# A decode kernel with V as the stationary operand of P times V, and K and V in one pool of 8 KB units

## The chip, the cores and the metric

The kernel runs on one core of one Trainium2 chip. The metric is the device time of one execution in microseconds (us). Before the change the median of three runs was 325.77 us (324.56 to 330.94, the last of them slow); a fourth run makes it 326.71. In what follows PE is the tensor engine (PEld its weight loads), DVE the vector engine, ACT the scalar engine, POOL the GpSimd engine and SP the engine that issues the loads; "SPq" in the profile is SP's own queue of instructions.

Each run is fast or slow; a run over 1.5% above the fastest of the same kernel is slow. The profiled executions of all kernels below had a granted clock of 1.0 for the tensor engine (the share of its full clock that the profile records), with one exception that is named.

## The reference

Two layers, each an attention over a window of the cache and a gated feed-forward block. Both layers use the same weights and the same caches.

```python
def _A_ref(x, k_cache, v_cache, wq, wo):      # x: [4, 1, 448]; 16 query heads, 8 KV heads, Dh = 256
    W = min(4096, max(256, Sk // 4))          # Sk = 8192, so W = 2048
    q = (x @ wq) ...                          # [B, 16, 1, 256]
    k = k_cache[:, :, Sk - W:, :]             # each KV head serves two query heads
    v = v_cache[:, :, Sk - W:, :]
    p = softmax(q k^T * Dh**-0.5)
    return (p v) ... @ wo
def _B_ref(x, w_gate, w_up, w_down):
    return (silu(x @ w_gate) * (x @ w_up)) @ w_down
x = x + _A_ref(layernorm(x)); x = x + _B_ref(layernorm(x))    # and both once more
```

The unit of work is a *pair*: one token and one KV head in one layer, so 4 x 8 x 2 = 64 pairs. A pair needs 1 MB of K and 1 MB of V. For each token five K and five V are kept in SBUF, the on-chip memory, from the first layer to the second; the rest is loaded again. That makes 88 loads of 512 KB of K halves and 88 of V halves, and 104 MB of loads with the weights.

## The kernel before

A scheduler in Python orders the instructions of each engine once, at build time, from a duration for each operation: the second argument of `g.op` (for example 1.18 us for a transpose). At run time each engine works through its list in that order and waits where it has to.

K arrives with keys on the partitions and has to be transposed, because the kernel's score matmuls take it with Dh there. DVE does it in 32x32 blocks of 4-byte words (two bf16 each), 88 instructions of 1233 ns. The parts that matter, for one pair:

```python
NS = 2; NQ = 3; NY = 3                         # buffers of scores, of q, of outputs
half = [sb(f"half{s}", [128, 8 * DH], BF16) for s in range(15)]    # 15 buffers of 4 KB per partition: raw K, or V
KT = [sb(f"KT{s}", [128, 16 * DH], BF16) for s in range(6)]        # 6 buffers of 8 KB: K transposed
# --- K: load two halves, transpose each; runs of 32 words are written side by side ---
src = half[cell[0]][:, :].bitcast(UINT32).rearrange("p (l k s) -> p l k s", l=2, k=16)
dst = KT[ks][:, :].bitcast(UINT32).rearrange("p (k l r) -> p l k r", k=16, l=4)
g.op(DVE, 1.12 + 0.06, pos, ... e.transpose(dst[:, 2 * hf:2 * hf + 2], src) ...)
# --- scores: 32 weight loads of K, 8 columns of q each ---
last = e.matmul(Sb[s_][:, 8 * gg:8 * gg + 8], lhsT=kt[:, gg, ce // 2, ce % 2, :], rhs=qe[q_][:, ce, :, :], ...)
# --- maximum (DVE, PE, DVE), then exp on ACT, once per query head ---
g.op(SCA, 0.17, pos, ... praw[s_] = exp(Sb[s_] - max) ...)
# --- keys are in the order of the transposes; V's rows are in another. A permutation matmul, and a copy ---
g.op(PE, 0.03, pos, lambda e: e.matmul(Yb[p_][:, 64:96], lhsT=permb[:, :], rhs=praw[s_][:, :], ...))
g.op(PE, 0.03, pos, ... matmul with ones: the sum of the weights ...)
g.op(SCA, 0.13, pos, ... pT[p_] = copy of Yb[p_][:, 64:96], every weight twice ...)
# --- P times V: V moves, 256 columns; 16 matmuls, each in a tile of 32 columns ---
last = e.matmul(Yb[p_][32 * gg:32 * gg + 4, 256:512], lhsT=pT[p_][:, 4 * gg + 2 * hv + a, :, :]...,
                rhs=half[vs[hv][0]][:, 1024 * a + 256 * gg:1024 * a + 256 * gg + 256], ...)
# --- o as a bf16 part and what is left of it; a "flip" matmul turns both round and adds up the tiles ---
g.op(SCA, 0.28, pos, ... oh[p_] = copy of Yb[p_][:, 256:512] ...)
g.op(DVE, 0.4, pos, ... oh[p_] = oh[p_] * lomask - Yb[p_][:, 256:512] ...)
last = e.matmul(Yb[p_][:, 2 * dh:2 * dh + 2], lhsT=oh[p_]..., rhs=osel[:, :], ...)        # twice
g.op(DVE, 0.09, pos, ... oT = Yb[p_][:, 0:4] / sum ...)
```

## Time and profile before

| before | value | where it is read |
|---|---|---|
| span of the profiled run | 322.9 us | head of the page |
| PE / DVE / ACT busy | 72% / 60% / 22% | part 1 |
| K transposes | 88 of 1233 ns, 108.3 us | part 5 |
| P times V | 1024 matmuls, 70.0 us | part 5 |
| GB/s in 0-88, 88-274, 274-303 us | 385, 351, 208 | busy time by windows |

The page of the kernel before. The first line is part 1 (busy time, share of the span, instructions); then the GB/s of 40 equal slices of 8.1 us; then the chain of work that ended last, by engine and by line; then five groups of instructions (output<-input, shape, count, busy us, mean ns of one, idle time of the engine before them, and what ended most of it).

```profile
PE 232.6 (72%) x5728; PEld 169.7 (53%) x5728; DVE 192.6 (60%) x608; ACT 72.4 (22%) x289; POOL 84.9 (26%) x199
...
GB/s 277 399 407 392 393 396 397 391 396 397 391 362 308 338 368 346 400 362 309 301 272 373 375 351 405 355 365 339 277 359 377 357 386 391 277 140 305 5 0 5
...
DMA 38%; PE 34%; DVE 12%; SPq 7%; issue 5%; ACT 2%; POOL 0%; DVEq 0%
DMA half<-in_A_k_cache_dram 20%; DMA half<-in_A_v_cache_dram 12%; PE Y L677 11%; PE S L637 8%; DVE KT L617 6%; DMA wd_sb<-in_B_w_down_dram 5%; PE Z L473 4%; SPq L389 4%; PE A L724 3%; PE Z L514 3%; DVE oh L691 2%; PE Z L542 2%; SPq L609 2%; DVE small L652 2%; SPq L626 1%
...
L617 DVE STREAM_TRANSPOSE KT<-half 128x1024 uint32<-128x1024 uint32 x88 | 108.3, 1233 | 13.3 <-DMA half<-in_A_k_cache_dram 12.9
L637 PE MATMUL S<-qe,KT 128*128 128x8 bf16 x2048 | 64.6, 168 | 22.4 <-DVE KT L617 18.5
L677 PE MATMUL Y<-half,pT 128*4 128x256 bf16 x1024 | 70.0, 403 | 9.6 <-DMA half<-in_A_v_cache_dram 8.7
...
L691 DVE SCALAR_TENSOR_TENSOR oh<-oh,small,Y 128x256 bf16<-128x256 bf16 x64 | 30.1, 472 | 23.9 <-ACT oh L689 23.4
...
L697 PE MATMUL Y<-osel,oh 128*128 128x2 bf16 x128 | 13.3, 173 | 17.4 <-DVE oh L691 17.2
```

How to read this. No engine is full. The chain goes through loads, PE and DVE in turn, and the loads run at about 395 GB/s for the first 88 us and then, up to 274 us, between 272 and 405. The four lower groups are what the change aims at: PE waited 18.5 us for transposes ahead of its score matmuls, and 17.2 us for the subtraction of line 691 ahead of the flip, in which it was busy for another 13.3 us; the subtraction itself took DVE 30.1 us.

The same by stages, from the table of windows (stretch in us, its length, then the busy us of PE, PEld, DVE, ACT and POOL with their counts, the granted clock, the share of DMA, GB/s):

```profile
0.00:88.00 88.00, 44.31 (x1019) 31.70 (x1019) 45.82 (x148) 13.12 (x51) 18.14 (x47) 1.00 1.01 385
88.00:274.00 186.00, 148.95 (x3671) 106.85 (x3672) 124.72 (x369) 48.89 (x197) 54.36 (x122) 1.00 0.97 351
274.00:303.00 29.00, 26.15 (x711) 20.89 (x708) 16.01 (x61) 6.96 (x28) 8.71 (x22) 1.00 0.61 208
```

The first stretch is bound by loads (385 GB/s, DMA share 1.01). In the second there is something to win, since loads run at 351 instead of 395 GB/s; in the third PE is busy for 26 of 29 us.

### The profile page before, as it was taken

The numbers are of one execution on the slowest core, as the hardware profiler recorded it, in microseconds if no ns is written. First come the engines' busy times: TensorE is split into PE (matmuls) and PEld (weight loads), VectorE is DVE, ScalarE is ACT, GpSimd is POOL, SyncE is SP. The second block draws the span as 40 slices with busy tenths as digits, with TensorE's granted clock in tenths as the row PEclk, the third lists the DMA queues.
The fourth block names the chain that finished last, engine by engine and source line by source line (L and its number), as shares of the span: only waits on it lengthen the run. The fifth ranks groups of instructions, "written<-read, shape, count | busy, mean of one in ns | idle before, by whom it ended". The sixth has DMA issues, their size and how long they took to land.

```text
span 322.9 us, 12873 instructions
## 1 busy us (share of the span) xinstructions
PE 232.6 (72%) x5728; PEld 169.7 (53%) x5728; DVE 192.6 (60%) x608; ACT 72.4 (22%) x289; POOL 84.9 (26%) x199
## 2 busy tenths in 40 slices
PE   3654454446588788578796895679787959889875
PEld 2542322234476465366664653567555636686554
DVE  5386555652145778765447787855377874656332
ACT  1112111111022333211231322113223322123310
POOL 3312111112023223240233331313233413134221
DMA  7999999999999999999889999999899999748000
GB/s 277 399 407 392 393 396 397 391 396 397 391 362 308 338 368 346 400 362 309 301 272 373 375 351 405 355 365 339 277 359 377 357 386 391 277 140 305 5 0 5
DMA packets 42327, 105.27 MB, mean 326 GB/s; under 512 B 3096, under 2 KB 7200, under 8 KB 41888
## 3 DMA queue, kind: packets, MB, share of 16 engines
q1 hardware_dynamic: 42272, 104.45, 88.0%
q8 instruction: 45, 0.74, 0.9%
q14 instruction: 10, 0.08, 0.1%
HBM read 104.44 MB, written 0.00 MB: 323 GB/s over the span
## 4 chain that ended last, share of the span: by engine, by line
DMA 38%; PE 34%; DVE 12%; SPq 7%; issue 5%; ACT 2%; POOL 0%; DVEq 0%
DMA half<-in_A_k_cache_dram 20%; DMA half<-in_A_v_cache_dram 12%; PE Y L677 11%; PE S L637 8%; DVE KT L617 6%; DMA wd_sb<-in_B_w_down_dram 5%; PE Z L473 4%; SPq L389 4%; PE A L724 3%; PE Z L514 3%; DVE oh L691 2%; PE Z L542 2%; SPq L609 2%; DVE small L652 2%; SPq L626 1%
## 5 line engine op out<-in xcount | busy, mean ns | idle before, releaser
L617 DVE STREAM_TRANSPOSE KT<-half 128x1024 uint32<-128x1024 uint32 x88 | 108.3, 1233 | 13.3 <-DMA half<-in_A_k_cache_dram 12.9
L637 PE MATMUL S<-qe,KT 128*128 128x8 bf16 x2048 | 64.6, 168 | 22.4 <-DVE KT L617 18.5
L677 PE MATMUL Y<-half,pT 128*4 128x256 bf16 x1024 | 70.0, 403 | 9.6 <-DMA half<-in_A_v_cache_dram 8.7
L637 PEld LDWEIGHTS S<-qe,KT 128*128 128x128 bf16 x2048 | 59.7, 104 | 30.7 <-DVE KT L617 20.8
L687 POOL TENSOR_TENSOR small<-small 128x2 f32<-128x2 f32 x64 | 44.3, 696 | 113.5 <-DVE small L669 103.3
L656 ACT ACTIVATE praw<-S,small 128x16 bf16<-128x16 f32 x128 | 28.7, 279 | 84.6 <-DVE small L652 83.9
L691 DVE SCALAR_TENSOR_TENSOR oh<-oh,small,Y 128x256 bf16<-128x256 bf16 x64 | 30.1, 472 | 23.9 <-ACT oh L689 23.4
L689 ACT ACTIVATE oh<-Y 128x256 bf16<-128x256 f32 x64 | 24.6, 384 | 74.2 <-PE Y L677 74.2
L641 POOL TENSOR_TENSOR qe<-qc,qmask 128x64 bf16<-128x64 bf16 x64 | 18.6, 294 | 71.3 <-PE S L637 52.3
L677 PEld LDWEIGHTS Y<-half,pT 128*4 128x4 bf16 x1024 | 20.0, 94 | 21.8 <-DMA half<-in_A_v_cache_dram 11.5
L646 DVE TRANSPOSE_TENSOR_REDUCE pmax<-S 128x1 bf16<-128x32 f32 x64 | 13.4, 211 | 27.1 <-PE S L637 25.3
L724 PE MATMUL A<-oT,wo_sb 128*128 128x1 bf16 (+1 forms) x688 | 24.8, 166 | 6.4 <-DVE oT L702 6.1
L724 PEld LDWEIGHTS A<-oT,wo_sb 128*128 128x128 bf16 x688 | 22.2, 105 | 10.5 <-DVE oT L702 8.5
L697 PE MATMUL Y<-osel,oh 128*128 128x2 bf16 x128 | 13.3, 173 | 17.4 <-DVE oh L691 17.2
L652 DVE TENSOR_REDUCE small<-S 128x2 f32<-128x128 f32 x64 | 17.4, 282 | 10.4 <-PE S L649 8.3
L666 ACT ACTIVATE pT<-Y 128x64 bf16<-128x64 f32 x64 | 14.1, 222 | 40.7 <-PE Y L663 40.4
L697 PEld LDWEIGHTS Y<-osel,oh 128*128 128x128 bf16 x128 | 8.8, 111 | 27.0 <-DVE oh L691 24.5
L649 PE MATMUL S<-identb,pmax 128*128 128x128 bf16 x64 | 16.6, 284 | 4.5 <-DVE pmax L646 3.6
L473 PE MATMUL Z<-xn,wq_sb 128*128 128x1 bf16 (+1 forms) x480 | 15.6, 165 | 2.6 <-DMA wq_sb<-in_A_wq_dram 1.9
L473 PEld LDWEIGHTS Z<-xn,wq_sb 128*128 128x128 bf16 x480 | 14.3, 104 | 3.4 <-DMA wq_sb<-in_A_wq_dram 2.0
L669 DVE TENSOR_REDUCE small<-Y 128x2 f32<-128x32 f32 x64 | 11.0, 177 | 7.1 <-ACT pT L666 6.8
L440 POOL TENSOR_SCALAR st<-st 128x1 f32<-128x1 f32 x16 | 4.3, 267 | 41.2 <-DVE st L428 40.7
(76 smaller groups left out, 212.0 us busy)
## 6 DMA issues: line engine op xcount, KB each, us to landing
half<-in_A_k_cache_dram SPq DMA_DIRECT2D x88, 512.0 KB, 7.0
half<-in_A_v_cache_dram SPq DMA_DIRECT2D x88, 512.0 KB, 6.7
wo_sb<-in_A_wo_dram SPq DMA_DIRECT2D x8, 448.0 KB, 12.3
wq_sb<-in_A_wq_dram SPq DMA_DIRECT2D x3, 1024.0 KB, 6.9
wd_sb<-in_B_w_down_dram SPq DMA_DIRECT2D x1, 1568.0 KB, 16.3
wg_sb<-in_B_w_gate_dram SPq DMA_DIRECT2D x1, 1344.0 KB, 14.2
wu_sb<-in_B_w_up_dram SPq DMA_DIRECT2D x1, 1344.0 KB, 14.7
wq_sb<-in_A_wq_dram SPq DMA_DIRECT2D x1, 512.0 KB, 10.4
```

Source lines behind the costliest of these rows:

```text
L473: last = e.matmul(o, lhsT=lhsT, rhs=rhs, start=(cc == 0 and hh == 0 and ee == 0), stop=(cc == 3), skip_group_check=True)
L617: return e.transpose(dst[:, 2 * hf + q * n:2 * hf + q * n + n], src[:, q * n:q * n + n])
L637: last = e.matmul(Sb[s_][:, 8 * gg:8 * gg + 8], lhsT=kt[:, gg, ce // 2, ce % 2, :], rhs=qe[q_][:, ce, :, :], start=(gg == 0 and ce == 0), ...
L641: g.op(POOL, 0.25, pos - SLEAD - 1, lambda e: e.tensor_tensor(qe[q_][:, :, :, :], qc[t][:, kvh, :, :].unsqueeze(2).broadcast_to([128, 8, 4 ...
L652: g.op(DVE, 0.2, pos, lambda e: e.tensor_reduce(negm[s_][:, :], Sb[s_][:, 128:256].rearrange("p (k n) -> p n k", n=2), AX.X, ALU.max, nega ...
L656: g.op(SCA, 0.17, pos, lambda e, n=n: e.activation(praw[s_][:, :].rearrange("p (k n) -> p n k", n=2)[:, n, :], Sb[s_][:, 0:32].rearrange(" ...
L677: last = e.matmul(Yb[p_][32 * gg:32 * gg + 4, 256:512], lhsT=pT[p_][:, 4 * gg + 2 * hv + a, :, :].rearrange("p y n -> p (y n)"), rhs=half[ ...
L687: g.op(POOL, 0.25, pos, lambda e: e.tensor_tensor(ri[p_][:, :], rs[p_][:, :], expo[:, 1:3], op=ALU.pow), r=(f"rs{p_}", "expo"), w=(f"ri{p_ ...
L689: g.op(SCA, 0.28, pos, lambda e: e.activation(oh[p_][:, :], Yb[p_][:, 256:512], ACT.Copy), r=(f"y{p_}",), w=(f"oh{p_}",), bank=(f"Y{p_}",))
L691: g.op(DVE, 0.4, pos, lambda e: e.scalar_tensor_tensor(out=oh[p_][:, :], in0=oh[p_][:, :], scalar=lomask[:, 0:1], in1=Yb[p_][:, 256:512], ...
L697: last = e.matmul(Yb[p_][:, 2 * dh:2 * dh + 2], lhsT=oh[p_][:, :].rearrange("p (m e) -> p e m", e=2)[:, dh, :], rhs=osel[:, :], start=Fals ...
L724: last = e.matmul(Av[:, cc, sl], lhsT=wo_sb[:, 4 * kvh + k, c0:c0 + 128], rhs=oT[si % 2][:, k % 2, k // 2, 0:n], start=False, stop=False, ...
```

## The change

The intent: turn P times V round. V becomes the stationary operand and the two columns of weights move, so that the output comes out with Dh on the partitions, as the next matmul wants it. The copy of o, the subtraction and the flip fall away. The permutation matmul and its copy fall away too, because the transposes now write the keys in the order of V's rows, and exp writes the weights of P times V directly. For that, a transposed row no longer goes to words that lie side by side: its words go to every fourth one, 16 bytes apart. Raw K, transposed K and V share 14 units of 8 KB with a rotating spare, into which the next K is transposed. The q selection takes one matmul instead of four. The counts of buffers go from NS 2, NQ 3, NY 3 to 3, 2, 2.

The diff, cut to the pair (setup, scheduler, q selection and renamings are left out):

```diff
-        half = [sb(f"half{s}", [128, 8 * DH], BF16) for s in range(NPOOL)]
-        KT = [sb(f"KT{s}", [128, 16 * DH], BF16) for s in range(NKT)]
+        unit = [sb(f"unit{s}", [128, 16 * DH], BF16) for s in range(NUNIT)]
 ...
-                            dst = KT[ks][:, :].bitcast(UINT32).rearrange("p (k l r) -> p l k r", k=16, l=4)
+                        dst = unit[kc[0]][:, :].bitcast(UINT32).rearrange("p (k r l) -> p l k r", k=16, l=4)
 ...
-                        o = g.op(DVE, 1.12 / TRP + 0.06, pos, tr, ...)
+                    o = g.op(DVE, 1.2, pos, turn, r=(kk + "r" + str(hf),), w=(kk + str(hf), "spare"))
 ...
-                g.op(SCA, 0.17, pos, lambda e, n=n: e.activation(
-                    praw[s_][:, :].rearrange("p (k n) -> p n k", n=2)[:, n, :],
-                    ...
-            g.op(PE, 0.03, pos, lambda e: e.matmul(Yb[p_][:, 64:96], lhsT=permb[:, :], rhs=praw[s_][:, :], ...
-            g.op(SCA, 0.13, pos, lambda e: e.activation(pT[p_][:, :, :, :], Yb[p_][:, 64:96]... ACT.Copy), ...
+                g.op(SCA, 0.2, pos, lambda e, n=n: e.activation(
+                    pT[p_][:, :, n], Sb[s_][:, 0:32].rearrange("p (k n) -> p n k", n=2)[:, n, :], ACT.Exp, ...
 ...
-                for a in range(2):
-                    for gg in range(4):
-                        last = e.matmul(Yb[p_][32 * gg:32 * gg + 4, 256:512],
-                                        lhsT=pT[p_][:, 4 * gg + 2 * hv + a, :, :].rearrange("p y n -> p (y n)"),
-                                        rhs=half[vs[hv][0]][:, 1024 * a + 256 * gg:1024 * a + 256 * gg + 256], ...
+                for ag in range(8 * hv, 8 * hv + 8):
+                    a, gg = ag // 4, ag % 4
+                    v = unit[vc[0]][:, 256 * ag:256 * ag + 256].rearrange("p (m e) -> p e m", e=2)
+                    for dh in range(2):
+                        last = e.matmul(Yb[p_][:, 2 * dh:2 * dh + 2], lhsT=v[:, dh, :], rhs=pT[p_][:, 4 * gg + a, :], ...
 ...
-            g.op(SCA, 0.28, pos, lambda e: e.activation(oh[p_][:, :], Yb[p_][:, 256:512], ACT.Copy), ...
-            g.op(DVE, 0.4, pos, lambda e: e.scalar_tensor_tensor(
-                out=oh[p_][:, :], in0=oh[p_][:, :], scalar=lomask[:, 0:1], in1=Yb[p_][:, 256:512], op0=ALU.mult, ...
-            g.op(PE, 0.06, pos, flip, r=(f"oh{p_}", "osel"), w=(f"yo{p_}",), bank=(f"Y{p_}",))
```

Per pair, P times V goes from 16 weight loads and 16 matmuls of 256 columns to 32 weight loads and 32 matmuls of 2 columns.

## The prediction

> **What bounds it now.** Not one engine. The page gives PE 72%, DVE 60%, DMA queue 88%; the chain of waits is DMA 38%, PE 34%, DVE 12%. In time (busy time by windows):
> - 0-88 us: DMA-bound, 390-400 GB/s, PE about half busy.
> - 88-274 us: mixed. GB/s averages about 350 and dips to 277-315 around the FFN and q-projection blocks, where PE is 7.3-7.6 of 8 us busy. Loads wait for buffers freed late.
> - 274-301 us: loads starved (208 GB/s), PE 26 of 29 us busy.
> - 301-323 us: no loads.
> The 104.4 MB at 395 GB/s need 264 us; last landing is near 300 us, so some 30 us of transfer time is lost, then a 22 us tail.[...]
>
> **Removed per pair (64 pairs), durations by groups of instructions:** the permutation matmul (about 0.03 us of issue), the ACT copy to pT (222 ns), the ACT copy of o (384 ns), the DVE subtract (472 ns), two flip matmuls (0.13 us of loads). The chain exp to PV loses about 0.45 us, PV to o loses 1.2-1.3 us. DVE drops 30 us, ACT 39 us. PE sat idle 17.2 us before the flip (wait on DVE) and spent 13.3 us in it. The q selection: 24 matmuls instead of 96; its ACT copies move to DVE (estimate +5 us).
> **Changed:** PV goes from 16 matmuls of N=256 in four column tiles (1.02 us per pair) to 32 full-array weight loads with N=2. The score matmuls have that form: 32 loads in 0.93 us. So PV is nearly even, about 0.95 us. The transposes now write with a 16-byte stride; I assume 1.23 us stays.
> **Buffers:** with 5 K and 5 V held, streaming has 4 units (32 KB per partition) instead of one KT plus five halves (28 KB). A transpose no longer waits for the previous pair's scores to free the only KT (part of the 18.5 us PE waits for transposes), but units come free whole, a K only after its scores. In the issue order most loads after pair 30 wait for the same or earlier work than before. DMA bytes are unchanged.
>
> **On the critical path.** 0-88 us: nothing. From 88 us some 46 pairs run up to the last q-projection (before: 286 us); PE gains 0.25-0.4 us per pair, or 12-18 us, against 23 us of transfer loss that can be recovered; I count 13. The tail of 8 pairs runs at about 2.8 us per pair; PE issue alone needs about 2.6 (0.93 scores, 0.3 max, 0.1 sum, 0.95 PV, 0.5 out): 3-6 us.
>
> **Predicted: 305 us**, range 295 to 317. Faster by over 2%: 0.86; within 2%: 0.11; slower: 0.03.
>
> **What would show it.** PV group near 65 us busy, 30 ns pitch; DVE total near 167 us, ACT near 35; GB/s in 88-270 us near 370; last K/V landing near 280; last q-projection near 272; tail after it near 31 us; unchanged first 88 us.
>
> **What would make it wrong.** (1) Transposes slow down from the 16-byte stride[...]; no run yet shows it. At 1.5 us DVE would hold 190 us and the gain would shrink to a few us. (2) PV's sum-before-PV order still makes PE wait on DVE behind a transpose. (3) Two Y banks instead of three, or whole-unit release, starve the loads.

13 us from 88 us on and 3 to 6 us in the tail, off the profiled span of 322.9 us, give 304 to 307 us. The estimate of +5 us for the copies of q agrees with the 5.6 us that line 481 of before takes on ACT.

## The result, and the profile after

The median of four runs was 357.84 us (355.23 to 362.06, the highest of them slow), against 326.71 us for the kernel before. The ratio is 1.0966, with a 95% interval of 1.0895 to 1.1036: slower by close to 10%, where 6% faster had been predicted. Here and below a ratio is the mean time of one kernel's fast runs over that of the other's fast runs of the same rounds, so it is not quite the ratio of the medians that are quoted.

The page of the kernel after, the lines that answer to those of before:

```profile
PE 210.8 (60%) x6488; PEld 194.5 (55%) x6488; DVE 232.4 (66%) x565; ACT 31.1 (9%) x137; POOL 85.3 (24%) x199
...
GB/s 293 397 401 397 394 393 396 393 400 390 234 220 376 396 341 266 239 257 288 358 352 401 323 226 223 211 304 290 357 378 402 378 269 179 281 159 264 97 4 4
...
DVE 41%; PE 40%; issue 14%; DMA 3%; SPq 1%; ACT 0%; DVEq 0%
DVE unit L611 33%; PE S L629 12%; PE Y L669 12%; PE Z L507 4%; PE A L700 4%; PE Z L470 3%; DMA unit<-in_A_k_cache_dram 3%; PE Z L535 2%; DVE small L646 2%; DVE misc L680 1%; DVE small L659 1%; PE Z L418 1%; PE S L643 1%; DVE misc L640 1%; SPq L385 1%
...
L611 DVE STREAM_TRANSPOSE unit<-unit 128x1024 uint32<-128x1024 uint32 x88 | 176.4, 2004 | 2.2 <-DMA unit<-in_A_k_cache_dram 0.5
L629 PE MATMUL S<-qe,unit 128*128 128x8 bf16 x2048 | 65.3, 168 | 76.0 <-DVE unit L611 54.7
...
L669 PE MATMUL Y<-pT,unit 128*128 128x2 bf16 x2048 | 68.7, 166 | 14.4 <-issue 9.5
L669 PEld LDWEIGHTS Y<-pT,unit 128*128 128x128 bf16 x2048 | 64.9, 105 | 15.6 <-issue 10.6
```

The groups of the copy, the subtraction and the flip are gone, and ACT fell from 72.4 to 31.1 us, as planned. P times V is at 68.7 us, even with before, as planned. But a K transpose takes 2004 ns instead of 1233, the 88 of them 176.4 us instead of 108.3, and DVE, which was to fall by some 25 us to near 167, gained 40. The head of the chain moved from loads to DVE (41%, of which line 611, the transposes, alone has 33%), and PE's wait for transposes ahead of the scores grew from 18.5 to 54.7 us. By stage: from 16.8 to 35.9 us in the first 88 us, where the loads run as before, and from 1.7 to 18.8 us after them, where it counts. One more name has grown in the chain: "issue", time in which the engine waited for nothing that the profile shows, is at 14%; it was 5%. And ahead of the matmuls of line 669, 9.5 us of idle time ended with "issue".

The windows of the kernel after, in the same columns:

```profile
0.00:88.00 88.00, 36.52 (x1018) 32.95 (x1019) 57.23 (x138) 6.01 (x22) 17.33 (x46) 1.00 1.01 385
88.00:274.00 186.00, 120.26 (x3787) 111.41 (x3784) 131.58 (x299) 17.98 (x83) 47.53 (x107) 1.00 0.87 307
274.00:303.00 29.00, 17.34 (x525) 15.60 (x521) 21.29 (x44) 3.12 (x14) 7.57 (x16) 1.00 0.84 286
```

The loads of the first 88 us are as before. In the second stretch loads fall from 351 to 307 GB/s, and PE is busy for 120 us instead of 149. DVE is not full either (132 of 186 us). So it may not be throughput alone: the order of DVE's list may matter (e11 tests it). The timeline of the kernel after (start, length, engine, group, and in brackets the idle time before and what ended it) shows how:

```profile
213.18 1.97 DVE L611 STREAM_TRANSPOSE unit<-unit 128x1024 uint32<-128x1024 uint32 x1
...
215.00 0.22 DVE L659 TENSOR_REDUCE small<-Y 128x2 f32<-128x32 f32 x2
...
215.25 4.06 DVE L611 STREAM_TRANSPOSE unit<-unit 128x1024 uint32<-128x1024 uint32 x2
217.28 0.93 PEld L629 LDWEIGHTS S<-qe,unit 128*128 128x128 bf16 x32 [3.39 <-DVE unit L611]
```

The sum of a pair (line 659) became DVE's turn only at 215.00, after a transpose; two further transposes follow back to back, and PE stands still for 3.4 us until the first of these is done.

### The profile page after: what moved, and what is told of

It reads as the page before. It is cut to its first block, busy times and chain, and to the rows that moved or that the text cites. A ratio compares the mean times of both kernels' runs of the same rounds, so it can differ in the third digit from the quotient of the medians.

```text
span 353.3 us, 14277 instructions
## 1 busy us (share of the span) xinstructions
PE 210.8 (60%) x6488; PEld 194.5 (55%) x6488; DVE 232.4 (66%) x565; ACT 31.1 (9%) x137; POOL 85.3 (24%) x199
## 4 chain that ended last, share of the span: by engine, by line
DVE 41%; PE 40%; issue 14%; DMA 3%; SPq 1%; ACT 0%; DVEq 0%
DVE unit L611 33%; PE S L629 12%; PE Y L669 12%; PE Z L507 4%; PE A L700 4%; PE Z L470 3%; DMA unit<-in_A_k_cache_dram 3%; PE Z L535 2%; DVE small L646 2%; DVE misc L680 1%; DVE small L659 1%; PE Z L418 1%; PE S L643 1%; DVE misc L640 1%; SPq L385 1%
## 5 line engine op out<-in xcount | busy, mean ns | idle before, releaser
L611 DVE STREAM_TRANSPOSE unit<-unit 128x1024 uint32<-128x1024 uint32 x88 | 176.4, 2004 | 2.2 <-DMA unit<-in_A_k_cache_dram 0.5
L629 PE MATMUL S<-qe,unit 128*128 128x8 bf16 x2048 | 65.3, 168 | 76.0 <-DVE unit L611 54.7
L629 PEld LDWEIGHTS S<-qe,unit 128*128 128x128 bf16 x2048 | 60.5, 104 | 80.0 <-DVE unit L611 57.2
L669 PE MATMUL Y<-pT,unit 128*128 128x2 bf16 x2048 | 68.7, 166 | 14.4 <-issue 9.5
L669 PEld LDWEIGHTS Y<-pT,unit 128*128 128x128 bf16 x2048 | 64.9, 105 | 15.6 <-issue 10.6
L677 POOL TENSOR_TENSOR small<-small 128x2 f32<-128x2 f32 x64 | 44.2, 693 | 110.4 <-DVE small L659 109.6
L650 ACT ACTIVATE pT<-S,small 128x16 bf16<-128x16 f32 x128 | 28.0, 278 | 297.0 <-PE Y L669 161.0
L633 POOL TENSOR_TENSOR qe<-qc,misc 128x64 bf16<-128x64 bf16 x64 | 18.7, 294 | 113.2 <-PE S L629 65.1
L640 DVE TRANSPOSE_TENSOR_REDUCE misc<-S 128x1 bf16<-128x32 f32 x64 | 13.3, 208 | 35.7 <-PE S L629 31.8
L700 PE MATMUL A<-misc,wo_sb 128*128 128x1 bf16 (+1 forms) x688 | 25.0, 166 | 4.4 <-DVE misc L680 2.5
L700 PEld LDWEIGHTS A<-misc,wo_sb 128*128 128x128 bf16 x688 | 22.0, 105 | 8.1 <-DVE misc L680 6.6
L643 PE MATMUL S<-identb,misc 128*128 128x128 bf16 x64 | 16.2, 283 | 7.5 <-DVE misc L640 6.7
```

What stands on the lines that cost most here:

```text
L611: return e.transpose(dst[:, 2 * hf:2 * hf + 2], src.rearrange("p (l k s) -> p l k s", l=2, k=16))
L633: g.op(POOL, 0.25, pos - SLEAD - 1, lambda e: e.tensor_tensor(qe[q_][:, :, :, :], qc[t][:, kvh, :, :].unsqueeze(2).broadcast_to([128, 8, 4 ...
L640: g.op(DVE, 0.12, pos, lambda e: e.tensor_reduce(pmax[s_][:, :], Sb[s_][:, 0:32], AX.X, ALU.max, apply_transpose=True), r=(f"s{s_}",), w=( ...
L643: g.op(PE, 0.1, pos, lambda e: e.matmul(Sb[s_][:, 128:256], lhsT=pmax[s_][:, 0:1].broadcast_to([128, 128]), rhs=identb[:, :], start=True, ...
L650: g.op(SCA, 0.2, pos, lambda e, n=n: e.activation(pT[p_][:, :, n], Sb[s_][:, 0:32].rearrange("p (k n) -> p n k", n=2)[:, n, :], ACT.Exp, b ...
L669: last = e.matmul(Yb[p_][:, 2 * dh:2 * dh + 2], lhsT=v[:, dh, :], rhs=pT[p_][:, 4 * gg + a, :], start=False, stop=(ag == 15 and dh == 1), ...
```

## The experiments

Theory A: the stride of 16 bytes makes the instruction itself slower, and that is the whole loss. Theory B, its first rival: the instruction is slow because of what runs beside it (loads, matmuls), not because of its addresses. The expectations also name rivals by other letters; each says there what it means. D was formed after the first four runs: that PE runs out of instructions. Kernels that are wrong are marked. One warning first: with the reference's inputs the attention's output is far below the rounding of x in bf16, so the comparison with the reference cannot see an error there. I therefore computed each kernel's values off the chip with enlarged inputs (a simulation, not one of the runs; the error is that of what the kernel adds to x): it was about 1% for before, after, e2, e4, e6, e7, e10, e11, e13 and e14 (e12 is e6 again), 139% for e1 and 100% for e5.

### e1_contig_wrong: the change without the stride (wrong)

```diff
-dst = unit[kc[0]][:, :].bitcast(UINT32).rearrange("p (k r l) -> p l k r", k=16, l=4)
+dst = unit[kc[0]][:, :].bitcast(UINT32).rearrange("p (k l r) -> p l k r", k=16, l=4)
```

The keys come in the old order then, so V's rows get the wrong weights; the instructions are otherwise the same.

> The changed kernel with one edit: the transposes write their 32-element runs contiguously, as the kernel before does. Keys then come out in an order that V's rows do not have, so the RESULT IS WRONG ON PURPOSE; instruction order and sizes are the same as in the changed kernel. Theory A (the 16-byte write stride makes a transpose take 2.0 us instead of 1.23 us, and the vector engine becomes the bound): transposes back at 1.23 us, vector engine about 165 us busy, time about 305 us as predicted (298 to 315). Rival B (transposes are slow because source and target are units of the same pool, or because of the loads landing beside them): transposes stay near 2.0 us and the time near 358 us. Rival C (whole-unit release and two Y banks starve the loads): transposes at 1.23 us but the time still above 325 us.

Measured: 330.48 us (ratio to before 1.0214, 1.0141 to 1.0287). The page of e1, the chain and the transposes:

```profile
PE 40%; DMA 17%; DVE 15%; SPq 13%; issue 13%; ACT 1%; DVEq 0%
...
L611 DVE STREAM_TRANSPOSE unit<-unit 128x1024 uint32<-128x1024 uint32 x88 | 108.9, 1237 | 8.5 <-DMA unit<-in_A_k_cache_dram 7.4
```

The transposes are back at 1237 ns, DVE at 172.1 us, near the 167 predicted, and by the ratios (1.0966 to 1.0214) some 24 of the 31 us are gone. So the stride explains most of the loss. But what is left is still 2% slower than before (classed as unclear against the limit of 2%, but the interval excludes 1), and not 6% faster: A is not the whole of it. 13% of "issue" stay in the chain.

### e2_before_strided: the kernel before, with the stride alone

```diff
-dst = KT[ks][:, :].bitcast(UINT32).rearrange("p (k l r) -> p l k r", k=16, l=4)
+dst = KT[ks][:, :].bitcast(UINT32).rearrange("p (k r l) -> p l k r", k=16, l=4)
-e.matmul(Yb[p_][:, 64:96], lhsT=permb[:, :], rhs=praw[s_][:, :], ...)
+e.matmul(Yb[p_][:, 64:96], lhsT=identb[:, :], rhs=praw[s_][:, :], ...)
```

> The kernel before with the transposes writing at a stride of 16 bytes and the permutation matrix replaced by the identity, so the result stays right. Theory A: transposes at 2.0 us, vector engine near 260 us busy, time well above before; an estimate of 370 us (355 to 390), since this kernel has 30 us more vector work than the changed one. Rival B: transposes stay at 1.23 us and the time at 326 us. Rival C: transposes may slow, but the time rises by under 10 us, as the vector engine is not what bounds.

Measured: 355.37 us, ratio 1.0966 (1.0943 to 1.099), by chance the very ratio of the whole change. The page of e2:

```profile
DVE 54%; PE 28%; DMA 8%; issue 5%; ACT 3%; SPq 1%; POOL 0%
...
L617 DVE STREAM_TRANSPOSE KT<-half 128x1024 uint32<-128x1024 uint32 x88 | 174.3, 2001 | 5.4 <-DMA half<-in_A_k_cache_dram 5.3
```

The same stride slows the same instruction in the old kernel to 2001 ns, with the old buffers and the old P times V. The size expected, about 370 us, was too large, since part of the transposes' 66 us more fell into time in which DVE had been idle (the span grew by 30 us).

### e3_micro: the transposes alone, without any traffic (wrong)

DVE alone transposes 128x1024 words, six times for each stride of writing; nothing is loaded and no other engine works. It writes zeros as its result.

```python
for i in range(6): step(e.transpose(w16[:, :].rearrange("p (k r l) -> p l k r", k=16, l=4)[:, 0:2], s(src[:, 0:1024])))
# and the same with l = 2 (8 bytes), 8 (32), 16 (64), 32 (128); contiguous; with a stride of 32 bytes in reading; plain copies
```

> The vector engine alone, no loads and no tensor engine; the output is zeros, WRONG ON PURPOSE. Transposes of 128x1024 uint32 with write strides of 4 (two forms), 8, 16, 32, 64 and 128 bytes, one with a read stride of 32 bytes, and plain copies with write strides of 4, 8 and 16 bytes, six of each. Theory A: 1.23 us at 4 bytes and 2.0 us at 16 bytes without any traffic beside it. [...]8 bytes stays at 1.23 us and everything from 16 bytes on is 2.0 us. Rival B: all forms alike.

Measured (one look, 109.5 us). The page of e3, groups by line; in order: reading with a stride of 32 bytes, writing with a stride of 16, of 64, of 8, and contiguous:

```profile
L101 DVE STREAM_TRANSPOSE rd<-src 128x1024 uint32<-128x1024 uint32 x6 | 12.0, 2006 | 0.2
L93 DVE STREAM_TRANSPOSE w<-src 128x1024 uint32<-128x1024 uint32 x6 | 11.9, 1979 | 0.2
...
L97 DVE STREAM_TRANSPOSE w<-src 128x1024 uint32<-128x1024 uint32 x6 | 11.4, 1892 | 0.2
L91 DVE STREAM_TRANSPOSE w<-src 128x1024 uint32<-128x1024 uint32 x6 | 7.5, 1246 | 0.2
...
L87 DVE STREAM_TRANSPOSE w<-src 128x1024 uint32<-128x1024 uint32 x6 | 7.5, 1246 | 0.2
```

The instruction is as slow alone (1979 ns) as in the kernel: B falls. A stride of 8 bytes costs nothing (1246 ns), 16 bytes cost 0.73 us, 32 bytes 0.77 (2019 ns), 64 and 128 bytes a little less than that (1892 and 1907). Reading with a stride of 32 bytes costs as much. A plain copy goes from 694 ns at 4 bytes and 695 at 8 to 1073 at 16. So the step lies between 8 and 16 bytes, for the transpose and for the copy, and from 16 bytes on the transposes stay between 1.89 and 2.02 us, as the last forecast had it. Why the step lies there, no run shows.

### e4_vsplit: V in the order of the transposes, instead of the reverse (right values)

If the transposes must write contiguously, V's rows may be loaded in their order. Each V half then takes four transfers of 32 partitions.

```diff
-dst = unit[kc[0]]... "p (k r l) -> p l k r"
+dst = unit[kc[0]]... "p (k l r) -> p l k r"
-vsrc = A_v_cache[...].rearrange("(a q g) d -> q a g d", a=4, q=128)
+vsrc = A_v_cache[...].rearrange("(a r l g) d -> l r a g d", a=4, l=4, g=4)
+for lq in range(4): ... unit[vc[0]][32 * lq:32 * lq + 32, ...] <- vsrc[lq, :, 2 * hv:2 * hv + 2, :, :]
```

> The contiguous write made right: each half of V is loaded by four transfers of 32 partitions (128 KB each) instead of one of 128 partitions, so that V's rows lie in the order in which the keys come out. The result must be right. Theory A: as e1 if small transfers cost nothing, about 305 us; if the extra issues (264 x 2 more) or the smaller transfers cost load rate, up to 325 us. Rivals B and C: as for e1.

Measured: 431.23 us (two of the four runs slow), ratio of the fast ones 1.3144. The page of e4:

```profile
GB/s 309 403 272 268 261 250 241 245 245 267 324 242 180 253 256 302 296 255 235 261 284 275 270 297 288 250 184 257 247 243 236 244 292 275 247 257 157 230 70 3
...
DMA 45%; SPq 27%; PE 17%; issue 7%; DVE 4%; ACT 0%; DVEq 0%
```

From the third slice on the loads mostly run at 180 to 300 instead of 395 GB/s (249 over the whole span), and the chain is mainly loads and their issue. The transposes were fast again (1242 ns), so nothing was wrong with them; the repair costs more than the damage. V now came in 352 transfers of 128 KB to 32 partitions instead of 88 of 512 KB to 128. Whether their number, their size or the 32 partitions made them slow, this run does not separate.

### e5_moving_v: e1, with V moving again (wrong)

Here the 2% that e1 still lost are sought in P times V. Everything of the change stays but its form; the steps that bring the moved output into place are left out, so the result is wrong and the time is a lower bound.

```diff
-for dh in range(2):
-    last = e.matmul(Yb[p_][:, 2 * dh:2 * dh + 2], lhsT=v[:, dh, :], rhs=pT[p_][:, 4 * gg + a, :], ...)
+last = e.matmul(Yb[p_][32 * gg:32 * gg + 2, 256:512], lhsT=pT[p_][:, 4 * gg + a, :],
+                rhs=unit[vc[0]][:, 256 * ag:256 * ag + 256], ...)
```

> e1 (contiguous transposes) with V moving again: 16 matmuls of 256 columns per pair in place of 32 loads and matmuls of 2 columns, in the same pools, banks and order. The sums land where nobody reads them, RESULT WRONG ON PURPOSE; the steps after PV stay as short as in the changed kernel. Theory D (what is left of the loss in e1 is the tensor engine's instruction fetch: each 16 KB block of 256 instructions is fetched by a DMA[...], and a stream of 15 ns instructions runs dry for 1.5 us and more, 37 us of gaps in e1 against 11 us before): gaps inside a line fall to about 10 us, time falls from 330 to 315 us or less. Theory C (whole-unit release by the tensor engine, or the banks, starves the loads): time stays at 325 to 335 us.

Measured: 314.63 us, ratio 0.966 (0.9612 to 0.9708), against 1.0214 for e1, on another chip. The page of e5, the chain and the group of P times V:

```profile
PE 43%; DMA 22%; DVE 15%; SPq 14%; issue 5%; ACT 1%; DVEq 0%
...
L669 PE MATMUL Y<-unit,pT 128*2 128x256 bf16 x1024 | 71.0, 402 | 17.3 <-DMA unit<-in_A_v_cache_dram 11.4
```

The group of P times V is busy for 71.0 us, no less than with V stationary (68.7 us in the kernel after), and yet the whole is 16 us, or by the ratios 5.4%, faster than e1, which has the same steps after P times V and the same durations told to the scheduler. "Issue" falls from 13 to 5% of the chain. So the stationary form costs time that is not in the busy time of its group.

### e6_before_stat_v and e12_stat_v_again: the kernel before, with V stationary alone

```diff
-last = e.matmul(Yb[p_][32 * gg:32 * gg + 4, 256:512], lhsT=pT[p_]..., rhs=half[vs[hv][0]]..., ...)
+for dh in range(2):
+    last = e.matmul(Yb[p_][:, 2 * dh:2 * dh + 2], lhsT=v[:, dh, :], rhs=pT[p_][:, 4 * gg + 2 * hv + a, :], ...)
-(the copy of o, the subtraction, the flip)
```

> The kernel before with V stationary and nothing else: its own pools, its own contiguous transposes and its permutation matmul; o comes out transposed, so the ACT copy, the DVE subtract and the flip go. The result must be right. Theory D: the fetch gaps inside a line rise to 25 us or more and eat what the shorter chain gives, 315 to 335 us. Theory C: the PV form is sound and only the pools hurt, so 312 us or less.

Measured: 333.49 us (334.76, 333.52, 327.72, 333.46), most runs slow. Again as e12:

> e6 once more, the same kernel, as its runs spread too widely for a verdict. Theory D: 0 to 3% slower than the kernel before (326 to 335 us), with 25 us or more of gaps inside a line at the fetches, in spite of 54 us less work on the vector and scalar engines.

Measured: 329.79 us, ratio 1.0133 (1.008 to 1.0185). The page of e12, the chain and P times V:

```profile
PE 37%; DMA 28%; DVE 13%; issue 12%; SPq 6%; ACT 2%; POOL 0%; DVEq 0%
...
L679 PE MATMUL Y<-pT,half 128*128 128x2 bf16 x2048 | 67.6, 165 | 11.3 <-issue 7.4
```

DVE fell by 23.5 us to 169.1 and ACT by 24.9 us to 47.5; the subtraction, the copy of o and the flip are gone; and the kernel is still no faster, but 1.3% slower. "Issue" is 12% of its chain, where it was 5%.

### e7_before_banks: the kernel before, with the counts of buffers of after

```diff
-NS = 2
-NQ = 3
-NY = 3
+NS = 3
+NQ = 2
+NY = 2
```

> The kernel before with the changed kernel's bank split (3 score banks, 2 Y banks, 2 buffers of masked q). The result must be right. If the bank split is what hurts in e1: 332 us or more. If not: 320 to 329 us.

Measured: 329.52 us, ratio 1.0128 (1.0055 to 1.02), about 4 us. The counts of buffers in the third risk of the prediction cost that little in the old kernel.

### Where "issue" is: the trace of e1

The timeline of PE's weight loads in e1, 12 us from the middle (start, length, engine, group, in brackets the idle time before):

```profile
112.00 0.98 PEld L669 LDWEIGHTS Y<-pT,unit 128*128 128x128 bf16 x34
115.64 0.88 PEld L669 LDWEIGHTS Y<-pT,unit 128*128 128x128 bf16 x30 [2.66 <-issue]
...
118.82 0.48 PEld L669 LDWEIGHTS Y<-pT,unit 128*128 128x128 bf16 x15
121.55 0.53 PEld L669 LDWEIGHTS Y<-pT,unit 128*128 128x128 bf16 x17 [2.25 <-issue]
```

P times V stops within its own run of loads, where nothing it needs can be missing: after 34 loads for 2.66 us, and again after 15 for 2.25 us. From the records I counted the stops longer than 0.5 us in the middle of one line's instructions that coincide with a 16 KB transfer of the queue "q8 instruction". Mostly they are 254 to 256 instructions apart, counting loads and matmuls, or a multiple of that, and PE resumes 2.2 to 2.6 us after the transfer begins. There are 7 of them in before (10.7 us), 14 in after (23.3 us), 19 in e1 (37.0 us), 17 in e12 (31.8 us), and 4 in e5 (8.1 us). These sums depend a little on where a stop is said to begin: a second count of the records gave 7, 14, 21, 18 and 5 stops, of 9, 21, 35, 30 and 8 us. All this fits theory D: PE waits for its own instructions. The pages agree with the distances: the queue "q8 instruction" makes 45 transfers (0.74 MB) in before, where PE has 2 x 5728 loads and matmuls, 51 (0.84 MB) in e1 with 2 x 6488, and 43 (0.70 MB) in e5 with 2 x 5464, which is one of 16 KB to 254 or 255 instructions.

### e8_micro_pe: PE alone, in runs of one width (wrong)

Five runs of 896 pairs of weight load and matmul, with nothing to wait for: 2, 64, 128 and 256 columns with 128 columns of weights, then 256 columns in tiles of four columns.

```python
for i in range(896):
    last = e.matmul(acc[0][:, 0:2], lhsT=wv[:, i % 2, :], rhs=x[:, 0:2], start=(i == 0), stop=(i == 895), ...)
# and the same with 64, 128 and 256 columns, and in tiles of 32
```

> The tensor engine alone, no loads beside it, zeros as output, WRONG ON PURPOSE: 896 pairs of weight load and matmul each of 2, 64, 128 and 256 columns with full weights, then 896 of 256 columns in four column tiles with 4-column weights. Theory D: with 2 columns (pace about 30 ns a pair) a gap of 1 to 2 us once in 256 instructions; the gap shrinks as the pairs get longer[...] and is near nothing at 256 columns. If the gaps come from the loads' traffic instead, there are none here.

Measured (one look, 231.37 us). The timeline of PE in e8:

```profile
1.55 23.41 PE L77 MATMUL a<-x,w 128*128 128x2 bf16 x863 [1.55 <-DVE x L69]
25.13 1.02 PE L77 MATMUL a<-x,w 128*128 128x2 bf16 x33 [0.18 <-issue]
26.02 28.22 PE L79 MATMUL a<-x,w 128*128 128x64 bf16 x896
```

The stops are missing: the longest between matmuls is 0.34 us, and 896 pairs of 2 columns go through in 24.5 us, 27 ns a pair. The expectation failed. With no loads beside it PE was held up by 0.34 us at most; D had to be amended by a condition, and loads were the obvious one.

### e9_micro_pe_loads: the same, with loads beside it (wrong)

```diff
+for r in range(10): for t in range(4): for h in range(4):      # 160 loads of 512 KB of K, five in flight
+    e.dma_start(un[i][:, :], A_k_cache[t, h, ...]).then_inc(ld[i], 16)
```

> e8 (the tensor engine alone, five kinds of matmul) with 160 loads of 512 KB from K running beside it, five in flight at a time, read by nobody; zeros as output, WRONG ON PURPOSE. e8 showed almost no gaps without traffic, against what was expected there. Theory D, mended (a fetch of instructions[...] comes late behind them; a stream of 15 ns instructions cannot wait so long): gaps of 1 to 3 us once in 256 instructions at 2 columns, so 896 pairs take 33 us or more instead of 24; smaller at 64 columns, none at 256 columns. If there are no gaps here either, the traffic is not the cause.

Measured (one look, 263.92 us; granted clock 0.974). The timeline of PE in e9:

```profile
1.55 6.11 PE L79 MATMUL a<-x,w 128*128 128x2 bf16 x223 [1.55 <-DVE x L71]
11.43 3.55 PE L79 MATMUL a<-x,w 128*128 128x2 bf16 x128 [3.77 <-issue]
18.72 3.56 PE L79 MATMUL a<-x,w 128*128 128x2 bf16 x128 [3.74 <-issue]
23.82 3.56 PE L79 MATMUL a<-x,w 128*128 128x2 bf16 x128 [1.54 <-issue]
...
86.36 51.64 PE L83 MATMUL a<-x,w 128*128 128x128 bf16 x896
```

Now 2 columns take 40.6 us instead of 24.5, with six stops of 1.3 to 3.8 us, exactly 128 pairs, which are 256 instructions, apart. 64 columns take 44.2 us instead of 28.1, with six stops of 0.8 to 2.9 us. 128 columns take 51.5 us and 256 columns 97.9, without a stop. (The tiles ran when the loads were over.) So the stop appears where both hold: loads run, and 256 instructions last only 3.6 to 3.9 us. At 128 columns 256 instructions last 7.4 us, and there was no stop. The 16 KB transfers were not slower under loads, but later: beside the six stops at 2 columns they took 0.88 to 0.95 us, against 0.95 to 1.40 us in the same stretch of e8, and four of the six began only after PE had stopped. Why they began late, by waiting behind the loads, say, was not tested.

This can account for P times V having become a loss. By busy time the two forms are even, but the old one fills 1.09 us a pair (70.0 us over 64 pairs) with 32 instructions and the new one 1.07 us (68.7 over 64) with 64.

### e10_before_onecopy: the kernel before, without the subtraction (right values)

```diff
-pT[p_][:, :, :, :], Yb[p_][:, 64:96]... (every weight twice)
+pT[p_][:, :, :], Yb[p_][:, 64:96]...
-g.op(DVE, 0.4, pos, lambda e: e.scalar_tensor_tensor(out=oh..., in0=oh..., scalar=lomask..., in1=Yb[p_][:, 256:512], ...))
```

o goes once through bf16 instead of as two parts.

> The kernel before with V moving as it is, but o goes through bf16 once: the DVE subtract that keeps its low part is dropped, the flip adds the four row groups of the ACT copy. The result must be right within the reference's tolerance. It takes 30 us off the vector engine and about 0.6 us off the chain after PV without adding an instruction to the tensor engine. Theory D: this is where a gain was to be had: 316 to 322 us. If the chain after PV is worth nothing: 324 to 327 us.

Measured: 321.94 us, ratio 0.9883 (0.9827 to 0.994): 1.2% faster. DVE lost 25.7 us (192.6 to 166.9) and PE most of its wait ahead of the flip (17.2 to 6.0 us), and the whole gained 4 us. This is what a shorter chain after P times V was worth when PE keeps its pace.

### e11_after_told: the kernel after, with the true duration given to the scheduler (right values)

```diff
-o = g.op(DVE, 1.2, pos, turn, ...)
+o = g.op(DVE, 1.95, pos, turn, ...)
```

> The changed kernel whose ordering is told that a transpose takes 1.95 us instead of 1.2 us; the instructions are the same, only their order on each engine is worked out anew. If part of the loss is an order made for faster transposes: 345 us or less. If the vector engine's work itself is the loss: 352 to 360 us.

Measured: 337.78 us, ratio 1.0363 (1.0289 to 1.0437), against 1.0966. The page of e11, the chain and the transposes:

```profile
PE 31%; DMA 24%; SPq 19%; DVE 12%; issue 12%; POOL 1%; ACT 0%; DVEq 0%
...
L611 DVE STREAM_TRANSPOSE unit<-unit 128x1024 uint32<-128x1024 uint32 x88 | 177.5, 2018 | 10.2 <-DMA unit<-in_A_k_cache_dram 9.7
```

The transposes take 2018 ns still, DVE is as busy, and some 20 of the 31 us are gone; nothing but the order has changed, and line 611 falls from 33 to 8% of the chain. So of the stride's cost the larger part (1.0966 to 1.0363, where e1, without the stride, has 1.0214) was not DVE's missing time, but an order made for transposes of 1.2 us. In the timeline above they stand in front of the small steps that PE waits for.

### e13_units_moving and e14_units_moving_banks: what is left of the change when its costs are left out (right values)

e13 has the pool of units, the new q selection, contiguous transposes with the permutation matmul, V moving, and o through one copy and the flip. The SBUF that the permutation needs comes from an area of software DMA, of which its page shows no queue. e14 is the same with the old counts of buffers.

```diff
 (against after)
-dst = unit[kc[0]]... "p (k r l) -> p l k r"
+dst = unit[kc[0]]... "p (k l r) -> p l k r"
+(permutation matmul and copy to pT, V moving, copy of o, flip: as in e10)
 (e14 against e13)
-NS = 3; NQ = 2; NY = 2
+NS = 2; NQ = 3; NY = 3
```

> A candidate that should beat both kernels: the changed kernel's pools of 8 KB units with the rotating spare, but contiguous transposes with the permutation matmul, V moving (16 matmuls per pair), and o through bf16 once as in e10. The result must be right. It needs 1.4 KB more per partition, taken from a scratch area of the software DMA that this kernel does not use. If the pools are worth what e5 suggested (314.6 us without any step after PV) and the steps after PV cost little: 315 to 320 us. If e5's gain came from the missing steps and the pools give nothing: 321 to 328 us, no better than e10.

> e13 with the bank split of the kernel before (2 score banks, 3 Y banks, 3 buffers of masked q). e7 found the changed kernel's split 1.3% slower in the old kernel. If that carries over: 1% below e13. If the split costs nothing where the chain after PV is shorter: as e13.

Measured: e13 321.24 us, ratio 0.9855 (0.9798 to 0.9912); e14 320.53 us (315.12 to 321.81), ratio 0.9718 (0.9624 to 0.9811) from only two fast runs, as its times fall into two states. Both are below both kernels, e13 by 1.5% against before and e14 by 2.8% in its two fast runs (the median of all its six is 1.9% lower), but e13 hardly more than e10, which is the old kernel with one step dropped. By e13 the pool of units is worth little by itself.

## Why the prediction was wrong, point by point

The comparisons that the points below rest on, in ratios to the kernel before:

| kernel | what it isolates | ratio |
|---|---|---|
| after | the whole change | 1.0966 |
| e2 | the stride alone, in the old kernel | 1.0966 |
| e11 | the change, with an order made for the true duration | 1.0363 |
| e1 | the change without the stride (wrong values) | 1.0214 |
| e12 | V stationary alone, in the old kernel | 1.0133 |
| e7 | the counts of buffers alone, in the old kernel | 1.0128 |
| e10 | the old kernel without the subtraction (o once through bf16) | 0.9883 |
| e13 | the units, without the stride, V moving | 0.9855 |
| e5 | e1 with V moving, last steps left out (wrong values) | 0.966 |

**The step that failed first: "The transposes now write with a 16-byte stride; I assume 1.23 us stays."** It is 2.00 us (e2, e3, the kernel after). 88 times 0.77 us are 68 us of DVE. The prediction named this risk itself, but put it into a list of what might go wrong instead of into the sum, and sized it by a guess ("At 1.5 us DVE would hold 190 us and the gain would shrink to a few us"). The trace of before could not show a size, since no transpose in it writes with that stride. What was knowable is that the stride was new and its cost unmeasured, and a range of 295 to 317 with 3% for slower did not say so.

**Missing in the prediction: what the order does with a wrong duration.** The list of DVE had been made for transposes of 1.2 us. The prediction looked only at DVE's total. Told the duration, the same instructions run 20 us faster (e11); the total of DVE was never full (66%).

**The second step that failed: "PE gains 0.25-0.4 us per pair, or 12-18 us".** Without the stride (e1) the change was still 2% slower. The busy time of P times V was right (65 us predicted; the weight loads took 64.9, the matmuls 68.7), and so were DVE near 167 us (172.1 in e1) and ACT near 35 us (31.1). Wrong was taking busy time for all that P times V costs. Twice the instructions in the same time go with PE waiting at blocks of 256 instructions while loads run (e9 by itself; the stops counted in e1, e12 and after). With V moving e1 became 16 us faster without the last steps (e5), and some 9 us faster (330.5 to 321.2, from runs on different chips; the ratios to before are 1.0214 and 0.9855) with the right values and nearly all the steps that the change had wanted to save (e13). And the removed steps were worth less than 12 to 18 us: the subtraction about 4 us (e10), the others about 6 (e13 against e5, by the ratios, where e5 gives wrong values), an estimate of 10 together. Part of the waits that were to be saved, 7.8 of the 17.2 us ahead of the flip, lay in the first 88 us, where loads set the pace.

**The tail was right.** From the last matmul of the q projection to the end of the span the trace gives 37.0 us before and 32.9 after; 31 was predicted, a gain of 3 to 6 us. Most of that time there are no loads beside PE (4 GB/s from 330 us on), which fits the condition that e8 and e9 found.

**The first 88 us were right**, 385 GB/s in both windows. The GB/s after them were wrong (near 370 predicted, 307 measured; 340 in e1, where the transposes were fast, and 351 before, so the smaller part of the loss is not theirs).

**Buffers.** The third risk, the counts of buffers, cost 1.3% in the old kernel (e7). That PE waits behind a transpose, the second risk, happened (after the first 88 us, 4.8 us of PE's idle time ahead of P times V ended with the sum of line 659), but with transposes longer than the order assumed. Whole-unit release was not varied alone.

**What stays open.** e5, which should have had all the gains, took 314.6 us and not 305; about 10 us of the predicted gain were not found in any kernel. The effects do not add up exactly: e1 to e5 is 16 us with one pool, before to e12 is 4 us the other way with the other, with the gain of e10 in it. Whether the counts of buffers matter with the units stays open through e14's two states. And the connection between the stops of PE and the 16 KB transfers rests on counting in the traces and on e8 and e9; that they cause the 1.3% of e12 was argued from it, not shown by a kernel that differs in the fetch alone. A rival stays: every kernel here has an order of its own, and e11 shows that an order by itself can be worth 6%, so differences of 1 to 2% (e1, e7, e12) may be partly luck of the order. The 5.4% between e1 and e5, which are told the same durations, are less open to that.

## What to carry to other kernels

When a change alters only the addresses of an instruction, measure that instruction alone before summing up the rest: one micro kernel of a tenth of a millisecond (e3) would have shown 2.0 instead of 1.25 us. After any change of a duration, give the new one to whatever orders the instructions, or the order can turn a small loss into a large one, as between e11 (ratio 1.0363) and the kernel after (1.0966). And when two forms of a product are even in busy time, try the one with fewer and longer instructions while loads are running; here it was faster (e5 against e1, 5.4%).
